# A retention and squared-ReLU kernel on one core: the planner's costs, due times and priorities set anew

## Chip, cores, metric

One core of a Trainium2 chip runs the kernel. The metric is the device time of one execution in microseconds (us), from profiled and unprofiled executions of the same program; the median of the runs is compared.

## What is computed

The reference has two stages. `q`, `k`, `v` are (8 batches, 8 heads, 576 positions, 64) in float32; `w_in` is 512 x 2048, `w_out` is 2048 x 512.

```python
scores = scale * np.matmul(q, k.transpose(0, 1, 3, 2))
gamma = 1.0 - 2.0 ** (-5.0 - np.arange(H, dtype=np.float32))
rel = pos[:, None] - pos[None, :]
Dmat = np.where(rel >= 0, gamma[:, None, None] ** rel[None, :, :], 0.0)
ret = scores * Dmat[None, :, :, :]
attn_out = np.matmul(ret, v)
x = attn_out.transpose(0, 2, 1, 3).reshape(B * S, H * D)      # 4608 x 512
r = np.maximum(x @ w_in, 0.0)
out = (r * r) @ w_out                                          # 4608 x 512
```

## The kernel before

**Tiling.** The 4608 tokens are 36 units of 128 (each batch has four full units; the last 64 positions of two batches make a tail unit). Two units make a group, so there are 18 groups, g0 to g17. Retention is computed chunk by chunk: scores within a chunk (`psc`), masked (`rx` or `rT`), times v (`psO`), with a running state `R` that is fed from k times v (`psS`) and decays from chunk to chunk. VectorE scales `psO` into `xT` (f16), which feeds the second stage.

**Second stage of a group** (`add_ff`). `ph` = x @ w_in comes in 16 blocks of four 128x256 matmuls (L876); two blocks share one PSUM bank. ScalarE takes the relu (`rl`, L884) and squares it (`gT`, L894) for seven of eight banks (three in the last two groups); the rest is squared on VectorE (L896). The second product: g0 does it plainly, 2 x 16 matmuls of 512 columns with w_out (L916). From g1 on it is a Strassen product, seven products p1 to p7 of eight matmuls each (L973; issued in the order p1, p7, p6, p2, p5, p3, p4) instead of eight. It needs sums of halves of `gT` (tile `gS`, L946: s3 for p7, s2 in two halves for p6, s1 for p5, s4 for p3) and of halves of w_out (tile `wT`, L827, four of two halves each: t1 for p5, t2 for p6, t3 for p7, t4 for p4), all on VectorE.

**Loads.** SyncE loads q, k and v. Units 0 to 7 come as pairs, one 512 KB transfer for each of k, q, v and two units: `k0`, `q0`, `v0`, `k2` and so on to `v6` (tile `pair`, L316). GpSimd issues the weights, which are turned into f16 on the way: w0 to w3 are quarters of w_in, w4 to w7 quarters of w_out (L331). The order is `FIRST`: the six transfers of pairs 0 and 2, then w0 to w7, then pairs 4 and 6; w0 is made to wait for v0, and k4 for w5. The pairs are cast to f16 (`kx`, `qx`, L424; `vx`, scaled by position, L420), transposed on TensorE (`psT`, L439) and copied back (`kqT`, L450). From unit 8 on, GpSimd casts k and q (L371, L382) and scales v (L387), and a DMA transposes (L400).

**Order.** Every step is a task with an engine, a key (smaller goes first), a duration, tasks that it depends on, and counted resources (`ff` for the eight PSUM banks, `wst` for staging buffers and so on). `Schedule.emit` plays the tasks through with these numbers: whenever an engine is free it takes the task of the smallest key that is ready and has its resources. The instructions are then written in the order of these planned starts. On the chip each engine follows its list in order and waits at semaphores; the numbers of the plan set nothing but the order. A task ends for another engine after a latency: 0.25 us from TensorE, 0.12 from ScalarE, VectorE and GpSimd; a load's landing is the end of its SyncE task plus `after`, 2.1 us plus what `LAG` has for it.

**The parts that the change names.**

- `fill` (L257 to L260): 34 matmuls on a zero tile, `warm`, with key 10**6: TensorE runs one when nothing else is ready in the plan. Planned at 1.75 us for the first, 0.43 for the next 14, 0.216 for the rest.
- `add_gated` (L265): a task that waits for the k or v cast of a unit, if that unit is one of those from 8 on, since only `add_unit` reads `gate`. `make_tail_pool` (two GpSimd instructions) is gated to unit 4, so it waits for nothing; `tail_dec` then makes the tail's decay row on VectorE (`vdl_tail`) and, in the same call, an Exp on ScalarE.
- `add_weight` (L325): the issue on GpSimd (0.9 us), and a SyncE task of 2.75 us that stands for the transfer.
- `add_unit_pair`: which engine casts what. Pair 0: VectorE. Pair 2: k on GpSimd and ScalarE, q on VectorE and ScalarE. Pairs 4 and 6: k on ScalarE, q on GpSimd. Always v's first half on GpSimd and its second on VectorE.
- `add_wT`: the eight half sums of w_out; those of t1 wait for w4 and w5, all others for w4 to w7.
- `add_ff`, `add_strassen`: relu, square and the sums s1 to s4, with keys by place in the group; `BESIDE` = 1.1 us is the cost of the second half of s2, 0.5 that of the first, 0.8 that of s1, s3 and s4.
- `after_sums`: `fr2` is the state's decay on VectorE.

Of the kernel before, what the change touches and what calls it, by code (L numbers as in the profile page):

```python
# [15 lines left out]
class Schedule:  # L16
# [4 lines left out]
        self.count = dict(count)  # L21
        self.tasks = []

    def add(self, eng, key, dur, fn, deps=(), acq=(), after=None, lag=0.0):
        t = dict(eng=eng, key=key, dur=dur, fn=fn, acq=acq, n=len(self.tasks), users=[], free=[], lag=lag,
                 left=len(deps), ready=0.0, lat=self.LAT[eng] if after is None else after)
        for d in deps:
            d["users"].append(t)
        self.tasks.append(t)
        return t  # L30
# [11 lines left out]
    def emit(self):  # L42
        ready = {e: [] for e in self.LAT}
        busy = {e: False for e in self.LAT}
        events = []
        order = []
        seq = 0

        def push(at, what, t):
            nonlocal seq  # L50
            seq += 1
            heapq.heappush(events, (at, seq, what, t))
        for t in self.tasks:
            if t["left"] == 0:
                heapq.heappush(ready[t["eng"]], (t["key"], t["n"], t))
        now = 0.0
        while True:
            for e in ready:
                if busy[e]:
                    continue  # L60
                held = []
                while ready[e]:
                    item = heapq.heappop(ready[e])
                    t = item[2]
                    if all(self.count[r] >= t["acq"].count(r) for r in t["acq"]):
                        for r in t["acq"]:
                            self.count[r] -= 1
                        t["start"] = now
                        order.append(t)
                        busy[e] = True  # L70
                        push(now + t["dur"], "end", t)
                        break
                    held.append(item)
                for item in held:
                    heapq.heappush(ready[e], item)
            if not events:
                break
            now = events[0][0]
            while events and events[0][0] <= now + 1e-9:
                _, _, what, t = heapq.heappop(events)  # L80
                if what == "end":
                    busy[t["eng"]] = False
                    for w in t["users"]:

                        push(now + (0.0 if w["eng"] == t["eng"] else t["lat"]), "dep", w)
                    for g in t["free"]:
                        push(now + t["lat"], "free", g)
                elif what == "dep":
                    t["left"] -= 1
                    if t["left"] == 0:  # L90
                        push(now + t["lag"], "go", t)
                elif what == "go":
                    heapq.heappush(ready[t["eng"]], (t["key"], t["n"], t))
                else:
# [9 lines left out]
def kernel(  # L104
# [122 lines left out]
    SQ_ACT = (0, 1, 2, 3, 4, 5, 6)  # L227
    SPREAD = 0.1
    QL = 0.8
    BESIDE = 1.1  # L230
    PAUSE = 1.5
    PARTS = 1
    WT_KEY = 96
    URGENT = 40
    SQ_LATE = (1, 4, 6)
    JOIN = 5
    LAG = {"k4": 0.7, "q4": 0.5}
    LAG_T, LAG_O = 1.5, 5.0
    PAIRED = 8
    FIRST = ["k0", "q0", "v0", "k2", "q2", "v2", "w0", "w1", "w2", "w3", "w4", "w5", "w6", "w7", "k4", "q4", "v4", "k6", "q6", "v6"]  # L240
# [31 lines left out]
        nc.gpsimd.tensor_copy(out=iota_pt[0:64], in_=iota_p[0:64])  # L272
        nc.gpsimd.tensor_scalar(out=iota_pt[64:128], in0=iota_p[64:128], scalar1=-64.0, scalar2=None, op0=ALU.add)

    tail_pool = add_gated("POOL", 4, "v", 2.2, make_tail_pool)
    tail_dec = add("DVE", 0, 0.3, lambda: make_vdec("tail", tile_of["iota_pt"]), deps=[tail_pool])

    def dma_task(key, dur, fn, **kw):
# [46 lines left out]
    def add_weight(i):  # L325
        fb = i % 4

        def fn():
            src, dst = ((w_in[:, fb * 512:(fb + 1) * 512].rearrange("(m p) f -> p m f", p=P), w_in16[:, :, fb * 512:(fb + 1) * 512]) if i < 4 else
                        (w_out[fb * 512:(fb + 1) * 512, :].rearrange("(n p) m -> p n m", p=P), w_out16[:, fb * 4:(fb + 1) * 4, :]))  # L330
            tile_of["w", i] = nc.gpsimd.dma_start(out=dst, in_=src)  # L331
            if i == 0:
                behind(tile_of["w", i], tile_of["load", "v", 0])
        issue = add("POOL", -90 + i, 0.9, fn, deps=issues[-1:] or [loaded["v", 0]], lag=1.0 if issues else 0.0)
        issues.append(issue)
        t = add("SP", 0, 2.75, lambda: None, deps=last_load + [issue], after=2.1 + LAG.get(f"w{i}", 0.0))
        last_load[:] = [t]
        wcast[i] = [t]

# [63 lines left out]
    def add_unit_pair(u, base):  # L403
# [4 lines left out]
        for i, name in enumerate("kqv"):  # L408
            xs[name] = []
            for e in range(2):  # L410
                eng = ("DVE" if (e if name == "v" else lead) else "ACT" if name == "k" and u >= 4 or u == 2 and e else
                       "DVE" if name == "q" and u == 2 else "POOL")

                def fc(name=name, e=e, eng=eng):
                    if (name + "x", u) not in tile_of:
                        tile_of[name + "x", u] = cast.tile([P, 2, H * D], FP16, name=name + "x", tag="kq16")
                    t = tile_of[name + "x", u][:, e]
                    x = tile_of[name + "32", u][:, :, e * D:(e + 1) * D]
                    if name == "v":
                        (nc.vector if eng == "DVE" else nc.gpsimd).tensor_tensor(  # L420
                            out=t.rearrange("p (h d) -> p h d", d=D), in0=x,
                            in1=vdec[f"pair{e}"].rearrange("p (h o) -> p h o", o=1).to_broadcast([P, H, D]), op=ALU.mult)
                    else:
                        engines[eng](out=t.rearrange("p (n b a d) -> p n b a d", n=2, b=2, a=2),  # L424
                                     in_=x.rearrange("p (a n b) d -> p n b a d", n=2, a=2))
                dur = (dict(POOL=1.1, DVE=0.6) if name == "v" else dict(POOL=0.62, DVE=0.4, ACT=0.59))[eng]
                xs[name].append(add(eng, base + (7 if name == "v" else i + e / 2), dur, fc, deps=[loaded[name, u]],
                                    acq=() if e else ("kq",)))
            if xs[name][0]["eng"] == xs[name][1]["eng"]:
                sched.need(xs[name][1], xs[name][0])  # L430
# [270 lines left out]
    def after_sums(g, t, key, res):  # L701
# [21 lines left out]
        if not c0:  # L723
            T["Rread", g - 1].append(r0)
        r1 = add("DVE", key + 0.2 - URGENT, 0.69, fr1, deps=[r0])
        r2 = add("DVE", key + 0.3, 0.65, fr2, deps=[r1], acq=("R",))
        T["Rm", g], T["R", g], T["Rread", g], T["Rmread", g] = r0, r2, [], r1
        sched.free("ff", [r0])
        sched.free("ff", [r1])
# [92 lines left out]
    def add_wT(i, in0, in1):  # L822
        ts = []
        for h in range(2):
            def f(h=h):
                sl = slice(h * HF // 2, (h + 1) * HF // 2)
                nc.vector.tensor_tensor(out=wT[i][:, sl], in0=in0[:, sl], in1=in1[:, sl], op=ALU.subtract)  # L827
            ts.append(add("DVE", WT_KEY + i, 0.7, f, deps=sum((wcast[j] for j in range(4, 8 if i else 6)), [])))
        return ts

    t1 = add_wT(0, wB[0, 1], wB[0, 0])
# [1 line left out]
    t3 = add_wT(2, wB[1, 1], wB[0, 1])  # L833
    t4 = add_wT(3, wB[1, 0], wT[1])
    for x, y in ((t2, t1), (t4, t2)):
        for p in y:
            for w in x:
                sched.need(w, p)
    wT_done = {7: t3, 6: t2, 5: t1, 4: t4}

    def store(u, o, lo=0, hi=DM, engs=(nc.sync, nc.sync)):
# [16 lines left out]
    def add_ff(g):  # L858
# [10 lines left out]
        for fb in range(NF // nf):  # L869
# [18 lines left out]
            def fg(fb=fb, on_act=on_act):  # L888
# [5 lines left out]
                    nc.scalar.activation(out=t, in_=rl, func=ACTF.Square)  # L894
                else:
                    nc.vector.tensor_tensor(out=t, in0=rl, in1=rl, op=ALU.mult)  # L896
            r = add("ACT", place(4 * fb + 4), 0.6, fr, deps=[f1[-1]], acq=("rl",))
            sched.free("ff", [r])
            sq.append(add("ACT" if on_act else "DVE", place(4 * fb + 6), 0.63 if on_act else 0.55, fg, deps=[r] + sq[:1],
                          acq=() if fb else ("g",)))  # L900
            sched.free("rl", [sq[-1]])
        sched.free("x", [f1[-1]])
        base2 = base + NF * n
# [28 lines left out]
    def add_strassen(g, us, base, sq):  # L932
# [7 lines left out]
        def add_sum(k, key, parts, in0, in1, op, deps, start=()):  # L940
            out_ = []
            for h in range(parts):
                def f(sl=cut(parts, h)):
                    if ("S", g) not in tile_of:
                        tile_of["S", g] = stage.tile([P, 4, HF, P], FP16, name="gS", tag="wst")
                    nc.vector.tensor_tensor(out=tile_of["S", g][:, k, sl], in0=in0(sl), in1=in1(sl), op=op)  # L946
                out_.append(add("DVE", key + h, (BESIDE if h else 0.5) if parts > 1 else 0.8, f, deps=deps(h, parts) + list(start)))
            sums[k] = out_
            return out_
        nb = len(sq) // 2  # L950
# [161 lines left out]
```

## Time and profile before

| what | us |
|---|---|
| runs (five), median, lowest to highest | 289.64, 289.35 to 290.06 |
| the profiled execution | 289.64 |
| its span, first to last instruction | 287.8 |
| TensorE busy in the span | 281.2 |
| VectorE, ScalarE, GpSimd busy | 178.7, 187.4, 86.3 |
| first `ph` matmul (L876) starts | 17.75 |
| granted TensorE clock, mean | 0.998 |
| weights w_in, w_out, issue to landing (median) | 9.0, 14.0 |

In the profile, lines such as L876 are lines of the kernel. A row of the timeline has the start and the duration in us, the engine, the line, the operation, the tiles it writes and reads with their sizes, and how many instructions were joined; in brackets how long the engine had been idle and what ended that. "PE" is TensorE's matmul row, "PEld" its loading of stationary operands, DVE VectorE, ACT ScalarE, POOL GpSimd. A row of waits has the waiting step, what it waited for, us in total, times, and the longest.

### The profile page before, as it was taken

The numbers are of one execution on the slowest core, as the hardware profiler recorded it, in microseconds if no ns is written. First come the engines' busy times: TensorE is split into PE (matmuls) and PEld (weight loads), VectorE is DVE, ScalarE is ACT, GpSimd is POOL, SyncE is SP. The second block draws the span as 40 slices with busy tenths as digits, with TensorE's granted clock in tenths as the row PEclk, the third lists the DMA queues.
The fourth block names the chain that finished last, engine by engine and source line by source line (L and its number), as shares of the span: only waits on it lengthen the run. The fifth ranks groups of instructions, "written<-read, shape, count | busy, mean of one in ns | idle before, by whom it ended". The sixth has DMA issues, their size and how long they took to land.

```text
span 287.8 us, 10135 instructions
## 1 busy us (share of the span) xinstructions
PE 281.2 (98%) x4346; PEld 236.2 (82%) x4346; DVE 178.7 (62%) x341; ACT 187.4 (65%) x363; POOL 86.3 (30%) x124
## 2 busy tenths in 40 slices
PE   7999999999999999999999999999999999999994
PEld 3578767888888888888888888888888888888883
DVE  3772379858666766547657674777666566364632
ACT  5559975667585857657576748575848675847830
POOL 5560035443524333433334433352522000000000
PEclk9999999999999999999999999999999999999999
DMA  7999999999999898999999897989888020102004
GB/s 199 276 208 206 247 287 274 177 241 156 254 198 165 226 236 187 206 180 189 212 182 224 186 207 177 248 181 246 160 216 205 5 77 2 73 2 75 0 4 144
DMA packets 122156, 49.94 MB, mean 173 GB/s; under 512 B 94720, under 2 KB 117760, under 8 KB 122112
## 3 DMA queue, kind: packets, MB, share of 16 engines
q1 hardware_dynamic: 117568, 44.84, 72.1%
q0 software_dynamic: 4224, 4.19, 8.8%
q8 instruction: 34, 0.56, 0.8%
q10 hardware_dynamic: 320, 0.26, 0.4%
q14 instruction: 10, 0.08, 0.1%
HBM read 36.70 MB, written 9.44 MB: 160 GB/s over the span
## 4 chain that ended last, share of the span: by engine, by line
PE 94%; POOL 2%; issue 2%; DVE 0%; POOLq 0%; DVEq 0%
PE ph L876 44%; PE po L973 37%; PE psO L357 5%; PE po L916 2%; PE psS L357 2%; PE psc L357 2%; PE warm L256 1%; PE psT L439 1%; POOL mask L216 0%; POOL vx L420 0%; POOL w_in L331 0%; DVE o L996 0%; POOL mask_full L208 0%; POOL mask_tail L208 0%; DVE p L1025 0%
## 5 line engine op out<-in xcount | busy, mean ns | idle before, releaser
L876 PE MATMUL ph<-xT,w_in 128*128 128x256 f16 x1152 | 136.5, 273 | 0.0
L876 PEld LDWEIGHTS <-w_in 128*128 128x128 f16 x1152 | 111.4, 98 | 14.4 <-DMA w_in<-in_moe_w_in_dram 0.3
L884 ACT ACTIVATE rl<-ph 128x512 f16<-128x512 f32 x144 | 84.3, 586 | 50.2 <-PE ph L876 47.6
L894 ACT ACTIVATE gT<-rl 128x512 f16<-128x512 f16 x118 | 74.4, 631 | 3.4
L973 PEld LDWEIGHTS <-gS 128*128 128x128 f16 x544 | 51.6, 98 | 6.5
L973 PE MATMUL po<-wT,gS 128*128 128x256 f16 x408 | 55.8, 273 | 0.0
L946 DVE TENSOR_TENSOR gS<-gT,gS 128x512 f16<-128x512 f16 (+1 forms) x51 | 30.7, 601 | 22.0 <-ACT gT L894 21.4
L973 PEld LDWEIGHTS <-gT 128*128 128x128 f16 x408 | 39.6, 98 | 4.7
L973 PE MATMUL po<-w_out,gT 128*128 128x256 f16 x272 | 36.7, 273 | 0.0
L387 POOL TENSOR_TENSOR v<-v,vdec_full 128x512 f16<-128x512 f32 x24 | 25.7, 1070 | 17.5 <-DMA v<-in_v_dram 11.4
L946 DVE TENSOR_TENSOR gS<-gT 128x1024 f16<-128x1024 f16 x34 | 26.2, 772 | 6.4 <-ACT gT L894 6.3
L371 POOL CAST kq<-k 128x512 f16<-128x512 f32 x28 | 19.2, 685 | 36.7 <-DMA k<-in_k_dram 33.0
L382 POOL CAST kq<-q 128x512 f16<-128x512 f32 x24 | 16.3, 679 | 38.8 <-DMA q<-in_q_dram 38.8
L896 DVE TENSOR_TENSOR gT<-rl 128x512 f16<-128x512 f16 x26 | 12.4, 477 | 20.6 <-ACT rl L884 20.6
L996 DVE TENSOR_TENSOR o<-po,u 128x256 f32<-128x256 f32 x33 | 13.9, 422 | 15.3 <-PE po L973 7.7
L986 ACT COPY u<-po 128x256 f32<-128x256 f32 x34 | 12.5, 368 | 15.7 <-PE po L973 15.5
L751 DVE TENSOR_TENSOR xT<-psO,gam_full 128x512 f16<-128x512 f32 x28 | 18.0, 685 | 4.3 <-PE psO L357 4.1
L996 DVE TENSOR_TENSOR o<-po,p 128x256 f32<-128x256 f32 x18 | 7.6, 424 | 20.6 <-ACT u L986 12.6
L973 PE MATMUL po<-w_out,gS 128*128 128x256 f16 x136 | 18.0, 273 | 0.0
L973 PE MATMUL po<-wT,gT 128*128 128x256 f16 x136 | 17.6, 273 | 0.0
L692 DVE TENSOR_TENSOR rT<-psc,mask_full 128x512 f16<-128x512 f32 x24 | 15.6, 683 | 3.1 <-PE psc L357 2.9
L1047 ACT COPY o<-po 128x256 f32<-128x256 f32 x16 | 5.9, 370 | 10.6 <-PE po L973 8.8
(82 smaller groups left out, 227.2 us busy)
## 6 DMA issues: line engine op xcount, KB each, us to landing
out_dram<-o SPq DMA_DIRECT2D x32, 256.0 KB, 2.8
k<-in_k_dram SPq DMA_DIRECT2D x24, 256.0 KB, 4.2
q<-in_q_dram SPq DMA_DIRECT2D x96, 64.0 KB, 3.2
v<-in_v_dram SPq DMA_DIRECT2D x24, 256.0 KB, 3.3
pair<-in_k_dram SPq DMA_DIRECT2D x4, 512.0 KB, 6.5
pair<-in_q_dram SPq DMA_DIRECT2D x4, 512.0 KB, 7.3
pair<-in_v_dram SPq DMA_DIRECT2D x4, 512.0 KB, 7.0
w_in<-in_moe_w_in_dram POOLq DMA_DIRECT2D x4, 512.0 KB, 9.0
```

Source lines behind the costliest of these rows:

```text
L357: t = nc.tensor.matmul(out_, lhsT=lhsT, rhs=rhs, start=start, stop=True, skip_group_check=True, tile_position=(64 * row, 64 * col))
L371: op(out=out_.rearrange("p (n b a d) -> p n b a d", n=2, b=2, a=2), in_=in_.rearrange("p (a n b) d -> p n b a d", n=2, a=2))
L382: nc.gpsimd.tensor_copy(out=tile_of["kq", u][:, 1].rearrange("p (t a d) -> p a t d", t=4, a=2), in_=tile_of["q32", u].rearrange("p (a t) d ...
L387: nc.gpsimd.tensor_tensor(out=t, in0=tile_of["v32", u], in1=vdec[kind].rearrange("p (h o) -> p h o", o=1).to_broadcast([P, H, D]), op=ALU. ...
L692: tile_of["masking", g] = nc.vector.tensor_tensor(out=tile_of["rT", g][:, :, a], in0=tile_of["psc", g][a].rearrange("p (s n i) -> p s n i" ...
L751: nc.vector.tensor_tensor(out=tile_of["x", g].rearrange("p n (s e i) -> p e (n s) i", s=n, e=2)[:, c], in0=y.rearrange("p (o t r) -> p o r ...
L876: nc.tensor.matmul(tile_of["ph", g, fb][:, j, :], lhsT=w_in16[:, m, fi * P:(fi + 1) * P], rhs=tile_of["x", g][:, m, :], start=(m == 0), st ...
L884: nc.scalar.activation(out=t, in_=tile_of["ph", g, fb], func=ACTF.Relu)
L894: nc.scalar.activation(out=t, in_=rl, func=ACTF.Square)
L946: nc.vector.tensor_tensor(out=tile_of["S", g][:, k, sl], in0=in0(sl), in1=in1(sl), op=op)
L973: nc.tensor.matmul(tile_of["pb", g, bank], lhsT=left(i), rhs=right[:, i, :], start=(start and i == 0), stop=(i == HF - 1), skip_group_chec ...
L996: nc.vector.tensor_tensor(out=o_tile(u)[:, half * HM:(half + 1) * HM], in0=bank(x), in1=tile_of[name, g], op=ALU.add)
```

## The change

It alters no instruction's form, only the engine of some casts, the point of one gate, and the planner: its costs, landings, priorities and how it counts VectorE beside GpSimd. What its name says of q's rows and of 34 fillers is in the kernel before already (L316, L225).

- `emit` gets `soft` tasks, on VectorE: while a GpSimd task of over 0.5 us runs, a soft task goes forward at 0.22 of its rate. Soft are the decay `fr2`, the sums for wT, VectorE's squares, and s1 to s4; their costs become 0.62, 0.68, 0.43, and 0.43 (halves) or 0.72.
- A weight chunk is planned at 2.58 us with 3.0 us to landing; `LAG` has new values.
- The tail's constants are gated to the scaling of v of unit 8, which `add_unit` does.
- Pair 2: k and q are cast on ScalarE alone.
- A half of wT waits only for the chunks that it reads, and a dependent half only for its own half.
- In g1 the last bank's relu, VectorE's square, and the sums s1 to s4 get a key that is smaller by `HURRY` = 60.

```diff
+    SHARED = 0.22
...
+        port = dict(task=None, left=0.0, at=0.0, beside=False)
+
+        def shared(beside):
+            t = port["task"]
+            if t is not None:
+                port["left"] -= (now - port["at"]) * (self.SHARED if port["beside"] else 1.0)
+                port["at"] = now
+                t["end"] = now + max(port["left"], 0.0) / (self.SHARED if beside else 1.0)
+                push(t["end"], "end", t)
+            port["beside"] = beside
...
-                        push(now + t["dur"], "end", t)
+                        t["end"] = now + t["dur"]
+                        if t["soft"]:
+                            port.update(task=t, left=t["dur"], at=now)
+                            shared(port["beside"])
+                        else:
+                            push(t["end"], "end", t)
+                        if e == "POOL" and t["dur"] > 0.5:
+                            shared(True)
...
+                    if t["soft"]:
+                        port["task"] = None
+                    elif t["eng"] == "POOL" and t["dur"] > 0.5:
+                        shared(False)
...
-    BESIDE = 1.1
+    HURRY = 60
...
-    LAG = {"k4": 0.7, "q4": 0.5}
+    LAG = {"k0": 0.3, "q2": 0.1, "w7": 1.4, "k4": 0.3, "q4": 0.7, "v4": 0.6, "q6": 0.3, "v6": 1.0}
...
-    tail_pool = add_gated("POOL", 4, "v", 2.2, make_tail_pool)
+    tail_pool = add_gated("POOL", 8, "v", 0.45, make_tail_pool)
...
-        t = add("SP", 0, 2.75, lambda: None, deps=last_load + [issue], after=2.1 + LAG.get(f"w{i}", 0.0))
+        t = add("SP", 0, 2.58, lambda: None, deps=last_load + [issue], after=3.0 + LAG.get(f"w{i}", 0.0))
...
-                eng = ("DVE" if (e if name == "v" else lead) else "ACT" if name == "k" and u >= 4 or u == 2 and e else
-                       "DVE" if name == "q" and u == 2 else "POOL")
+                eng = ("DVE" if (e if name == "v" else lead) else "ACT" if name == "k" and u >= 4 or u == 2 and name != "v" else "POOL")
...
-        r2 = add("DVE", key + 0.3, 0.65, fr2, deps=[r1], acq=("R",))
+        r2 = add("DVE", key + 0.3, 0.62, fr2, deps=[r1], acq=("R",), soft=True)
...
-            ts.append(add("DVE", WT_KEY + i, 0.7, f, deps=sum((wcast[j] for j in range(4, 8 if i else 6)), [])))
+            ts.append(add("DVE", WT_KEY + i, 0.68, f, deps=wcast[4 + h] + (wcast[6 + h] if i else []), soft=True))
...
-        for p in y:
-            for w in x:
-                sched.need(w, p)
+        for w, p in zip(x, y):
+            sched.need(w, p)
...
-            r = add("ACT", place(4 * fb + 4), 0.6, fr, deps=[f1[-1]], acq=("rl",))
+            r = add("ACT", place(4 * fb + 4) - HURRY * (g == 1 and fb == 7), 0.6, fr, deps=[f1[-1]], acq=("rl",))
...
-            sq.append(add("ACT" if on_act else "DVE", place(4 * fb + 6), 0.63 if on_act else 0.55, fg, deps=[r] + sq[:1],
-                          acq=() if fb else ("g",)))
+            sq.append(add("ACT" if on_act else "DVE", place(4 * fb + 6) - HURRY * (g == 1 and not on_act), 0.63 if on_act else 0.43, fg, deps=[r] + sq[:1],
+                          acq=() if fb else ("g",), soft=not on_act))
...
-                out_.append(add("DVE", key + h, (BESIDE if h else 0.5) if parts > 1 else 0.8, f, deps=deps(h, parts) + list(start)))
+                out_.append(add("DVE", key + h - HURRY * (g == 1), 0.43 if parts > 1 else 0.72, f, deps=deps(h, parts) + list(start), soft=True))
```

More of the change, by code (lines that the diff above doesn't have):

```diff
@@ L22, in __init__, with add @@
         self.tasks = []
-    def add(self, eng, key, dur, fn, deps=(), acq=(), after=None, lag=0.0):
-        t = dict(eng=eng, key=key, dur=dur, fn=fn, acq=acq, n=len(self.tasks), users=[], free=[], lag=lag,
+    SHARED = 0.22
+    def add(self, eng, key, dur, fn, deps=(), acq=(), after=None, lag=0.0, soft=False):
+        t = dict(soft=soft, eng=eng, key=key, dur=dur, fn=fn, acq=acq, n=len(self.tasks), users=[], free=[], lag=lag,
                  left=len(deps), ready=0.0, lat=self.LAT[eng] if after is None else after)
@@ L81, in emit @@
                 if what == "end":
+                    if abs(t["end"] - now) > 1e-6:
+                        continue
+                    t["end"] = -1.0
                     busy[t["eng"]] = False
+                    if t["soft"]:
+                        port["task"] = None
+                    elif t["eng"] == "POOL" and t["dur"] > 0.5:
+                        shared(False)
                     for w in t["users"]:
```

## Prediction

> **What bounds the kernel now.** I read the page's first two parts, then busy time by stage, then TensorE's waits, and last the timeline of the first 50 us beside the landing records of the transfers.
>
> ```profile
> PE 281.2 (98%) x4346; PEld 236.2 (82%) x4346; DVE 178.7 (62%) x341; ACT 187.4 (65%) x363; POOL 86.3 (30%) x124
> ...
> PE   7999999999999999999999999999999999999994
> ```
>
> TensorE (PE) is busy in every slice but the first and the last. By stage (columns: PE, PEld, DVE, ACT, POOL, clock, DMA share, GB/s):
>
> ```profile
> 1.26:17.75 16.49, 15.63 (x234) 7.90 (x235) 11.09 (x44) 8.13 (x19) 11.34 (x27) 1.00 1.12 249
> 17.75:51.73 33.98, 33.80 (x471) 25.65 (x465) 21.45 (x37) 25.61 (x48) 9.41 (x13) 1.00 1.15 246
> 51.73:284.00 232.27, 231.72 (x3650) 202.61 (x3647) 145.60 (x255) 153.25 (x296) 65.00 (x81) 1.00 0.76 160
> 284.00:287.90 3.90, 0.00 (x0) 0.00 (x0) 0.24 (x1) 0.00 (x0) 0.00 (x0) 0.81 0.34 82
> ```
>
> From 17.75 us, the first `ph` matmul, to 284 us PE lacks 0.72 us of full, mostly the change between 64-row and 128-row work. Up to 17.75 it is busy too, but 11.01 of those 15.63 us are the 34 fillers `warm`; the DMA engines are full there. Its only named waits:
>
> ```profile
> PE warm L256 <- DVE wT L163: 1.3, 1, 1.3
> PE psS L357 <- POOL vx L420: 0.4, 1, 0.4
> PE psT L439 <- DVE kx L424: 0.2, 1, 0.2
> ```
>
> So time = real matmuls + 34 fillers + PE's idle time + 3.9 us behind the last matmul. The change touches neither the matmuls nor the number of fillers: only idle time can change. About 1 us can be removed ahead of 17.75 us, and 0.15 us at 19.5 us, where PE waits for w1. Much more can be added. The profiled execution took 289.64 us (span 287.85 and 1.8 around it), just the median, so the sum is set against 289.64.
>
> **Ahead of the first ph: nothing.** k0 landed at 5.07 us, yet its cast began at 5.86, as `vdl_tail` stood ahead of it on VectorE and waited for GpSimd. The new gate moves this away and the cast can start 0.7 us sooner. But two later steps hold PE (timeline):
>
> ```profile
> 10.05 1.04 POOL L420 TENSOR_TENSOR vx<-pair,vdec_pair 128x512 f16<-128x512 f32 x1
> ...
> 11.14 0.45 PE L357 MATMUL psS<-vx,kx 64*64 64x64 f16 x32 [0.45 <-POOL vx L420]
> ...
> 14.22 1.45 POOL L420 TENSOR_TENSOR vx<-pair,vdec_pair 128x512 f16<-128x512 f32 x1 [1.06 <-DMA pair<-in_v_dram]
> ...
> 15.72 0.45 PE L357 MATMUL psS<-vx,kx 64*64 64x64 f16 x32
> ```
>
> Both psS begin when GpSimd's vx is done, and vx hangs on the landings of v0 (8.69) and v2 (14.05), which the change leaves alone. I worked PE's new order by hand from the planner's costs: 12 fillers instead of 11 before the first transpose, then 2 instead of 3, and 5 instead of 4 before psc; that is 21 ahead of the first psS, as before, then 9 up to the second (3, 5, 1 instead of 5, 2, 2), then 4. The same counts between the same holds: ph again begins at 17.7. The cast of pair 2 moving to ScalarE (four of 0.62 us, 2.5 in sum, in place of two) is hidden: its k casts end by 11.75, its transposes come at 12.2, and q's copies end near 16.4 with psc at 17.06. Without that cover it would cost at most the 0.6 us of one cast.
>
> **Weights: +0.49 us.** In the planner w(i) landed at 11.95 + 2.75(i+1) + 2.1 us; now 11.95 + 2.58(i+1) + 3.0. That makes w1 20.11 instead of 19.55, w3 25.27 instead of 25.05, w5 30.43 instead of 30.55. The trace has w1 at 19.60, w3 at 24.97, w5 at 30.46. The new plan thus lets PE rest 0.63 us ahead of w1; on the chip that rest is the present 0.15 us, and PE then runs ahead of the plan and meets w3 and w5 too early. Counting the blocks (four matmuls of 109 ns, 0.437 us) that the plan puts ahead of w5's first matmul: before, 9 of g1 (2 ahead of w3, 2 ahead of w4, 5 ahead of w5); now 1, 2 and 4, that is 7. All other work ahead of it is the same.
>
> ```profile
> 30.89 1.03 PE L916 MATMUL po<-w_out,gT 128*128 128x512 f16 x4
> ```
>
> This is w5's first use. It could have begun at 30.51 (landing and 0.05, as w1's first matmul at 19.65 stood to 19.60): 0.38 us of slack. Two blocks less are 0.87 us, so 0.49 us becomes idle, some 0.27 of it at w3. The bounds: 0 if the weights land half a microsecond sooner, 0.9 if later by as much.
>
> **Third pair: +0.2 and -0.2.** With wT's halves tied to single chunks and g1's last sums hurried, VectorE's list at 36 to 42 us gets shorter, and the transposes of k4 move from plan time 40.0 to 38.7. From w5 on PE needs 0.86 + 1.75 + 0.86 + 2.18 + 2.37 us to reach them (38.5; their casts end by about 38.3), then 0.45 + 1.30 + 0.45 + 0.65 + 0.66 + 0.09 to psS: 42.1. GpSimd's vx ended at 42.26 in the trace and has the same landing to wait for: 0.2 us idle (0 to 0.6; if GpSimd's q casts also lengthen beside wT, PE waits there instead). Against it, psS and psc of the fourth pair come to lie side by side: one change of row mode less, 0.09 + 0.12 us by the gaps around psS at 42.9. The hurried relu is no cost by itself: ScalarE does as many instructions.
>
> **Tail constants moved.** Two GpSimd instructions (0.18 + 0.22), one on VectorE (0.23) and one Exp on ScalarE (0.30) go from 5 us to about 53. Behind them wait unit 9's cast, VectorE's backlog, and on ScalarE the relus of g2, which run without gap from 52.80 to 61. ScalarE also waits for VectorE there, up to 1 us. Who waits for it: p1 and the sums of g2, used 1.7 us or more after they were ready. I take zero; 0.5 if that cover were half gone. In the trace the Exp stood among copies without a second table load.
>
> **From 52 us on: +0.2 us.** The plan charged 1.1 us for the second half of s2 and 0.55 for the square ahead of it; now 0.43 each, slowed to 0.22 beside GpSimd. In the timeline the second half of p6 began 0.5 to 1.8 us (mostly 1.2 to 1.7) after its sum was ready; 0.67 + 0.12 us of that was this margin. Beside GpSimd the sums take longer:
>
> ```profile
> 74.45 1.04 POOL L387 TENSOR_TENSOR v<-v,vdec_full 128x512 f16<-128x512 f32 x1 [1.07 <-DMA v<-in_v_dram]
> ...
> 74.53 1.24 DVE L946 TENSOR_TENSOR gS<-gT,gS 128x512 f16<-128x512 f16 x1 [1.74 <-ACT gT L894]
> ```
>
> 1.24 instead of 0.43: the rate gives 0.43 + 0.78 x 1.04 = 1.24. The Trainium skill (SBUF — State Buffer, Who interferes with whom) speaks against a rate: two-input VectorE work and a GpSimd read exclude each other, and the one that comes second waits wholly. That would be 0.96 + 0.43 = 1.39 here, and nothing for a VectorE op that comes first, as with the sum at 57.79 (0.68 with GpSimd beside it all through). So the plan is right where GpSimd leads and too slow where VectorE does; the second only moves PE's work back, which costs nothing. What costs is a GpSimd op that comes at another time than planned. With 0.8 us less margin, some 0.4 to 0.9 are left; a square or sum that meets GpSimd loses up to 0.8. For a quarter of the 12 groups with GpSimd work and a shortfall of 0 to 0.2 I take 0.2 us in all, bounds 0 and 2. By the lock alone it would be about 0.1 more.
>
> Sum: 0 + 0.49 + 0.18 - 0.21 + 0 + 0.2 = 0.66, that is 290.3 us.
>
> **Rivals.** (a) Not slower, chance 0.23: w2 to w5 land sooner. GpSimd no longer casts k2 between the issues of w1 and w2, so w2 is issued at about 11.85 instead of 12.41. If that fills the weights' queue, w5 lands by 29.97 and the 0.49 is gone: 289.64 + 0.18 - 0.21 = 289.6, decided at that landing. Against it: w2 landed 2.5 us after w1 and 9.7 after its issue; the bytes, not the issue, set the pace. (b) Faster, 0.13: the earlier k0 cast carries through, vx of pair 2 is shorter (1.04 as elsewhere, not 1.45), and ph begins at w0's landing, 17.25: 289.1 or less. Against it: w3 and w5 then hold PE the longer. (c) Clearly slower, 0.22: the lost margin counts in most groups, 12 x 0.15 = 1.8 and the rest: 291.5. For it: 12 of the 34 half sums ran beside GpSimd, 0.2 us longer on average. (d) That the change does nothing is part of (a).
>
> **How the numbers follow.** My own case has 0.42 and reaches from 289.95 to 290.7. What a measurement can tell from no change is about 0.2%, 0.58 us: 289.06 to 290.22. Two thirds of my case lie above it (0.28), and all of (c): slower 0.50. One third of mine and (a): same 0.37. (b): faster 0.13. The range 289.2 to 291.9 leaves out half of (b) and the far end of (c).
>
> **What would show it.** Right: PE's list of waits gains `ph` on w_in near 24.7 us and `po` L916 on w_out near 30.3, together about 0.5; ph still starts at 17.7; kx starts at 5.1; psS at 42.3 right behind vx; gaps of PE at L973 behind gS below 0.3 us in all. Wrong: ph starting before 17.4; a gapless stretch from 20 to 40 us; PE waits on VectorE beyond 1 us behind 52 us; a first ph of g2 before 51.7 or after 53.

## The result, and the profile after

The changed kernel takes 290.26 us (median; 289.87 to 291.07) against 289.69 us for the kernel before, run beside it. The ratio is 1.0019, 95% interval 1.0013 to 1.0025: slower by about 0.2%, at the edge of what can be told from no change. The profiled executions are 289.64 before and 290.12 after, their spans 287.85 and 288.41. The prediction was 290.3. All ratios are those on record, which leave out the four executions that were in a slow state and are not the quotients of two medians: the two differ by up to 0.3% (e3: 1.0049, by medians 1.0078), so small steps between experiments have to be read with care.

The page after, first two parts (lines of the new kernel stand 25 to 27 further down: `ph` L901, plain `po` L941, Strassen `po` L998, quads L384, sums `gS` L971):

```profile
PE 281.2 (98%) x4346; PEld 236.0 (82%) x4346; DVE 179.7 (62%) x340; ACT 188.2 (65%) x365; POOL 87.4 (30%) x123
...
PE   8899999999999999999999999999999999999994
```

PE's work is what it was, 281.2 us. Busy time by stage (same columns as before):

```profile
17.75:51.73 33.98, 33.19 (x463) 24.68 (x458) 21.05 (x37) 25.67 (x48) 9.32 (x15) 1.00 1.12 236
51.73:284.20 232.47, 232.19 (x3660) 203.29 (x3656) 146.94 (x255) 153.30 (x298) 67.05 (x81) 1.00 0.74 161
```

The loss lies in the first row: PE lacks 0.79 us there, 0.18 before. In the long stage behind 51.73 us it lacks 0.28, against 0.55. TensorE's waits after:

```profile
PE warm L283 <- DVE wT L190: 1.3, 1, 1.3
PE psS L384 <- POOL vx L446: 1.1, 2, 0.7
PE ph L901 <- DMA w_in<-in_moe_w_in_dram: 0.3, 1, 0.3
```

`warm` waits at the start as before. New are `ph` on w_in, and a second wait of psS on GpSimd's vx; the 0.2 us of `psT` is not in this list any more. Where they are (timeline of PE after):

```profile
17.74 2.36 PE L901 MATMUL ph<-xT,w_in 128*128 128x256 f16 x20
...
25.05 2.79 PE L901 MATMUL ph<-xT,w_in 128*128 128x256 f16 x24 [0.27 <-DMA w_in<-in_moe_w_in_dram]
...
30.29 1.03 PE L941 MATMUL po<-w_out,gT 128*128 128x512 f16 x4
...
42.36 0.45 PE L384 MATMUL psS<-vx,kx 64*64 64x64 f16 x32 [0.35 <-POOL vx L446]
...
43.28 0.42 PE L384 MATMUL psc<-kqT 64*64 64x128 f16 x16
43.63 0.39 PE L998 MATMUL po<-wT,gS 128*128 128x256 f16 x2
43.95 0.42 PE L384 MATMUL psc<-kqT 64*64 64x128 f16 x16
```

The same two steps of the third pair before:

```profile
42.94 0.45 PE L357 MATMUL psS<-vx,kx 64*64 64x64 f16 x32
...
44.07 0.64 PE L357 MATMUL psc<-kqT 64*64 64x128 f16 x32
```

`ph` starts at 17.74 (17.75 before). w3 landed at 25.00 and PE was there early: the bracket counts 0.27 us of idle time from the modelled end of the matmul ahead, and from start to start it is 0.54 us where two such matmuls otherwise stand 0.11 apart. w1 landed at 19.39 (19.60 before), and PE's wait for it, 0.15 us before, is gone. w5 landed at 30.13, not at 30.46, and its first product starts without a wait. The psS of the third pair stands behind vx. The score matmuls `psc` of that pair are cut in two by two `po`.

I summed TensorE's gaps from the start of one matmul to the start of the next, over each part of both traces. The last matmul starts 0.73 us later (283.46, 284.20):

| term | predicted | measured |
|---|---|---|
| ahead of the first ph | 0 | -0.01 |
| weights: gaps inside ph and po up to 40 us | +0.49 | +0.29 |
| psS of the third pair | +0.18 | +0.41 |
| row modes from 40 to 60 us: entering quads (64-row matmuls), and time in them | -0.21 | +0.19 - 0.10 |
| tail's constants | 0 | 0 |
| behind 60 us | +0.2 | -0.10 |
| sum | 0.66 | 0.68 |

The other 0.05 us is spread over short gaps of full matmuls between 40 and 60 us. The 0.29 is 0.43 at w3 less the 0.15 at w1. The -0.10 in row modes comes mostly from a wait: before, psS of the fourth pair stood about 0.2 us for VectorE's vx in its middle, and after it does not.

### The profile page after: what moved, and what is told of

Same layout as the page of the kernel before. It is cut to its first block, busy times and chain, and to the rows that moved or that the text cites. A ratio compares the mean times of both kernels' runs of the same rounds, so it can differ in the third digit from the quotient of the medians.

```text
span 288.4 us, 10133 instructions
## 1 busy us (share of the span) xinstructions
PE 281.2 (98%) x4346; PEld 236.0 (82%) x4346; DVE 179.7 (62%) x340; ACT 188.2 (65%) x365; POOL 87.4 (30%) x123
## 4 chain that ended last, share of the span: by engine, by line
PE 80%; DMA 9%; ACT 3%; SPq 2%; DVE 2%; POOL 2%; issue 0%; DVEq 0%; POOLq 0%; ACTq 0%
PE ph L901 37%; PE po L998 36%; DMA w_out<-in_moe_w_out_dram 5%; PE psO L384 4%; DMA pair<-in_v_dram 3%; DMA pair<-in_k_dram 2%; SPq L343 2%; PE psc L384 2%; PE psS L384 2%; ACT rl L909 1%; ACT gT L919 1%; POOL vx L446 1%; DVE rT L718 0%; ACT kx L450 0%; ACT kqT L476 0%
## 5 line engine op out<-in xcount | busy, mean ns | idle before, releaser
L901 PE MATMUL ph<-xT,w_in 128*128 128x256 f16 x1152 | 137.7, 273 | 0.3 <-DMA w_in<-in_moe_w_in_dram 0.3
L901 PEld LDWEIGHTS <-w_in 128*128 128x128 f16 x1152 | 111.3, 98 | 14.7 <-DMA w_in<-in_moe_w_in_dram 0.5
L998 PEld LDWEIGHTS <-gS 128*128 128x128 f16 x544 | 51.6, 98 | 6.8
L998 PE MATMUL po<-wT,gS 128*128 128x256 f16 x408 | 56.1, 273 | 0.0
L998 PEld LDWEIGHTS <-gT 128*128 128x128 f16 x408 | 39.7, 98 | 4.9
L971 DVE TENSOR_TENSOR gS<-gT,gS 128x512 f16<-128x512 f16 (+1 forms) x51 | 31.4, 617 | 19.6 <-ACT gT L919 19.1
L998 PE MATMUL po<-w_out,gT 128*128 128x256 f16 x272 | 36.9, 273 | 0.0
L414 POOL TENSOR_TENSOR v<-v,vdec_full 128x512 f16<-128x512 f32 x24 | 27.5, 1145 | 29.2 <-DMA v<-in_v_dram 23.8
L971 DVE TENSOR_TENSOR gS<-gT 128x1024 f16<-128x1024 f16 x34 | 27.2, 799 | 8.2 <-ACT gT L919 8.1
L998 PE MATMUL po<-w_out,gS 128*128 128x256 f16 x136 | 17.7, 273 | 0.0
L998 PE MATMUL po<-wT,gT 128*128 128x256 f16 x136 | 17.6, 273 | 0.0
L487 DVE TENSOR_TENSOR R<-stmp,dec 128x512 f16<-128x512 f32 (+1 forms) x18 | 13.0, 722 | 0.5
```

The lines of the kernel that those rows point to most:

```text
L414: nc.gpsimd.tensor_tensor(out=t, in0=tile_of["v32", u], in1=vdec[kind].rearrange("p (h o) -> p h o", o=1).to_broadcast([P, H, D]), op=ALU. ...
L901: nc.tensor.matmul(tile_of["ph", g, fb][:, j, :], lhsT=w_in16[:, m, fi * P:(fi + 1) * P], rhs=tile_of["x", g][:, m, :], start=(m == 0), st ...
L998: nc.tensor.matmul(tile_of["pb", g, bank], lhsT=left(i), rhs=right[:, i, :], start=(start and i == 0), stop=(i == HF - 1), skip_group_chec ...
```

## The experiments

They ran in three groups (e1 to e4, e5 to e8, e9 to e12), each group on one chip of its own, beside the kernel before on that chip; ratios are against that. "By the gaps" means: from the start of one matmul to the start of the next, less the usual step. The lists of waits leave out idle times under 0.15 us, the gaps do not. Two of the planner's halves were exchanged in turn: the landings (the transfer's 2.58 + 3.0 us and the new `LAG`, or the old 2.75 + 2.1 us), and VectorE's costs with the rate.

**e1: the kernel before with the new landings alone.**

```diff
-    LAG = {"k4": 0.7, "q4": 0.5}
+    LAG = {"k0": 0.3, "q2": 0.1, "w7": 1.4, "k4": 0.3, "q4": 0.7, "v4": 0.6, "q6": 0.3, "v6": 1.0}
-        t = add("SP", 0, 2.75, lambda: None, deps=last_load + [issue], after=2.1 + LAG.get(f"w{i}", 0.0))
+        t = add("SP", 0, 2.58, lambda: None, deps=last_load + [issue], after=3.0 + LAG.get(f"w{i}", 0.0))
```

> The kernel before with nothing of the change but the planned landings (2.58 and 3.0 us for a weight chunk, the new LAG). Landing theory (PE reaches w3, or w5, and the psS of the third pair before their data): the plan again has only 7 blocks of g1 ahead of w5's first matmul and psS at plan time 42.15, so the same two waits, 0.3 us at w3 and 0.4 us at psS: 290.3 us, ratio 1.002. Rate theory (the loss comes from VectorE's new costs and the lost margin behind 52 us): no loss, 289.7 us.

Measured 292.72 us, ratio 1.0079 (1.0061 to 1.0097): four times the loss of the whole change. In its timeline one step that nobody had looked at is the longest wait:

```profile
111.47 0.32 PE L357 MATMUL psc<-kqT 64*64 64x64 f16 x16 [1.20 <-DMA kqT<-kq]
```

The scores of a late group wait for their DMA transpose. A further 0.5 us is lost at `po` on VectorE's `xT` near 50 us. The new landings do cost time, but hardly where they were expected to: by the gaps w3 holds PE for 0.09 us and the third pair's psS not at all.

**e2: the changed kernel with the old landings** (the reverse of e1's edit).

> The changed kernel with the landings planned as before the change (2.75 and 2.1 us, old LAG); all other parts of the change stay. Landing theory: 9 blocks of g1 ahead of w5 again, psS at plan time 43.56, so no wait at w3 or psS beyond 0.15 us: 289.7 us, ratio 1.000. Rate theory: the loss stays, 290.3 us.

Ratio 0.9991 (0.9969 to 1.0013; 1.0011 by the medians): no loss is left that can be told from noise, as expected. Neither w3 nor the third pair's psS holds PE; other small waits stand in their place, the largest at 63 us, on ScalarE:

```profile
PE po L998 <- ACT p L1011: 0.7, 1, 0.7
PE psS L384 <- POOL vx L446: 0.5, 1, 0.5
```

The second row is the wait of pair 0, which before has too. By the gaps psS of the fourth pair stands 0.6 us for VectorE's vx, as it does in e9 and e12.

**e3: the changed kernel with pairs 4 and 6 planned later**, so that psS of the third pair would not come early.

```diff
-    LAG = {"k0": 0.3, "q2": 0.1, "w7": 1.4, "k4": 0.3, "q4": 0.7, "v4": 0.6, "q6": 0.3, "v6": 1.0}
+    LAG = {"k0": 0.3, "q2": 0.1, "w7": 1.4, "k4": 2.06, "q4": 1.86, "v4": 1.36, "k6": 1.36, "q6": 1.36, "v6": 1.36}
```

> The changed kernel with the landings of pairs 4 and 6 planned as late as in the plan of before (LAG raised by 1.4 to 2.1 us), the weights' landings left as changed. It undoes the wait at the third pair's psS alone. Landing theory: the wait at w3 (0.3 us) stays, that at psS (0.4 us) goes: 289.9 us, 0.2 to 0.3 above before. If the weights alone cost, 290.3; if neither does, also 290.3.

A miss: ratio 1.0049 (1.0028 to 1.0069). The wait at w3, which was to stay, is gone as well (PE stands at w1 instead, 0.46 us by the gaps). The third pair's wait is gone, and the fourth's takes its place, larger (first row: timeline; second: waits):

```profile
49.62 0.45 PE L384 MATMUL psS<-vx,kx 64*64 64x64 f16 x32 [1.27 <-POOL vx L446]
```

```profile
PE psc L384 <- DMA kqT<-kq: 2.1, 3, 1.0
```

Again the transposes, 2.1 us in three places.

**e4: the kernel before with 30 fillers** (`WARM = 30` instead of 34), for the prediction's claim that the fillers are not what bounds the start.

> The kernel before with 30 fillers for 34; the four that go are those between the second psS (15.72 us) and psc. If time were simply PE's matmuls and fillers, four of 0.216 us less: 288.8 us. Landing theory: ph starts 0.4 us sooner, at w0's landing, and then waits 0.6 us or more for w1 at 19.6 instead of 0.15: 289.7 us, no gain.

Ratio 0.9992 (0.9973 to 1.0011): four fillers, 0.86 us of PE, win nothing.

```profile
16.38 0.53 PE L357 MATMUL psc<-kqT 64*64 64x128 f16 x24 [0.21 <-ACT kqT L450]
17.43 0.30 PE L357 MATMUL psc<-kqT 64*64 64x128 f16 x7 [0.52 <-issue]
17.67 1.92 PE L876 MATMUL ph<-xT,w_in 128*128 128x256 f16 x16
19.90 1.48 PE L876 MATMUL ph<-xT,w_in 128*128 128x256 f16 x12 [0.32 <-DMA w_in<-in_moe_w_in_dram]
```

PE reaches psc sooner and waits there; ph starts at 17.67 and what is won, 0.08 us, is waited for again at w1. The long stand, 0.52 us, has no releaser in the trace. It falls ahead of the 224th matmul of PE's list, and in eight other traces (before, after, e2, e5, e6, e7, e9, e10) psc also pauses at just that place, with 0.09 to 0.21 us from start to start, though in e4 that is four score matmuls further on; in all nine the pause ends at 17.43 to 17.46. So something tied to the place in the list holds ph as well, beside the two psS of the prediction. What it is, no run here tests.

**e5: the changed kernel with w1 alone planned 0.45 us sooner**, so that the plan rests less ahead of w1 and puts one block more ahead of w5.

```diff
-    LAG = {"k0": 0.3, "q2": 0.1, "w7": 1.4, "k4": 0.3, "q4": 0.7, "v4": 0.6, "q6": 0.3, "v6": 1.0}
+    LAG = {"k0": 0.3, "q2": 0.1, "w1": -0.45, "w7": 1.4, "k4": 0.3, "q4": 0.7, "v4": 0.6, "q6": 0.3, "v6": 1.0}
```

> The changed kernel with one number changed: w1's landing planned 0.45 us sooner (19.66 us, as the trace has it). The plan then has no rest of 0.63 us ahead of w1, 8 blocks of g1 ahead of w5 and psS at plan time 44.0 instead of 42.15. Landing theory: both waits of the changed kernel (0.3 us at w3, 0.4 us at the third pair's psS) go, with this one number: 289.7 us, as before. Rate theory (VectorE's new costs lose it behind 52 us): 290.3.

Ratio 1.0020 (0.9999 to 1.0040), median 290.87: it cannot be told from before, nor from after. In the trace both waits, at w3 and at the third pair, are gone as they should be (that at w3 is gone in e3, e8 and e10 too, without this edit), but the profiled run (292.08, above this kernel's median) waits 1.6 us for transposes, in four places. The lowest run, 289.34, is level with before's lowest, 289.3.

**e6: the changed kernel with VectorE's old costs and no rate.** The costs of `fr2`, wT, the squares and the sums are before's, for instance:

```diff
-                out_.append(add("DVE", key + h - HURRY * (g == 1), 0.43 if parts > 1 else 0.72, f, deps=deps(h, parts) + list(start), soft=True))
+                out_.append(add("DVE", key + h - HURRY * (g == 1), (1.1 if h else 0.5) if parts > 1 else 0.8, f, deps=deps(h, parts) + list(start)))
```

> The changed kernel with VectorE's costs as before the change (0.55, 0.5 and 1.1, 0.8, 0.65, 0.7) and no slower rate beside GpSimd. PE's order up to plan time 46 is that of the changed kernel. Rate theory: the loss goes, 289.7. Landing theory: both waits stay, 290.3 at least; as the plan also rests PE 0.66 us at 50 us, PE would run ahead of the transposes of units 12 to 20, as in the runs with late landings: up to 291.

Ratio 1.0056 (1.0030 to 1.0082): slower than the change itself, by more than expected. The longest wait is on VectorE, at the end of g1:

```profile
52.67 0.60 PE L998 MATMUL po<-wT,gT 128*128 128x256 f16 x4 [1.06 <-DVE o L1021]
```

and 0.5 us on a transpose at 110. Neither of the two waits that were to stay is there: w3 and the third pair's psS do not hold PE, and w5's first product stands 0.29 us by the gaps. So beside the new landings the new costs are worth about 0.35% (1 us); they are not what makes the change slower.

**e7: e5 and e6 together.**

> Both at once: VectorE's costs as before the change, and w1's landing planned 0.45 us sooner. In this plan PE rests only 0.18 us behind 17.8 us (before 0.64, changed kernel 0.63). If what costs is a rest that the plan has and the chip has not, this is the best order so far: 289.4 to 289.7 us, no wait at w3, psS, or a transpose. Rate theory: 289.7. If margins decide more than rests, 290 or more.

Ratio 1.0008 (0.9982 to 1.0035), profile 289.9. No wait at w3 and none on a transpose; psS of the fourth pair waits 0.6 us for VectorE's vx. Level with before within the interval, without the gain that was expected.

**e8: the changed kernel without the rate** (`soft=False` throughout, the new costs kept).

> The changed kernel with its new VectorE costs (0.43, 0.72 and so on) but no slower rate beside GpSimd, so no margin at all is left for GpSimd. PE's order is that of the changed kernel up to 56 us. Landing theory: 290.3 us, as the changed kernel, with PE waits on VectorE of at most 0.3 us in sum. Rate theory (lost margin): slower by 0.5 us or more than the changed kernel, 290.8 to 291.5.

Ratio 1.0041 (1.0024 to 1.0058), 291.32: the number that the rate theory expected, by another way. By the list PE waits for VectorE nowhere behind the start (one sum holds it 0.08 us by the gaps); it waits for transposes:

```profile
PE psc L384 <- DMA kqT<-kq: 1.3, 2, 0.8
...
PE psS L384 <- POOL vx L446: 1.0, 2, 0.7
```

So the theory that the rate keeps VectorE's sums clear of GpSimd falls, though its time came out. What the costs and the rate change, as far as these traces show, is where the scores stand in PE's list.

**e9 and e10: the kernel before, and the changed kernel, unchanged, on one chip**, to tell whether the order or the chip makes the transposes late.

> The kernel before, unchanged, on the chip of this group, for its trace. Theory A (the order decides how early the DMA transposes are issued): the score matmuls of groups 6 to 10 find their transposes landed 1.5 us or more ahead, as in the first trace of before (1.5 to 4.4), and PE has no wait on kqT behind 52 us. Theory B (the chip decides): leads near zero and waits on kqT of 0.3 us or more, as in the runs of edited kernels. Time 289.7 (289.3 to 290.1 if nothing disturbs), ratio 1.000.

> The changed kernel, unchanged, beside before on one chip. Ratio 1.002 as measured (1.001 to 1.0035). Theory A: leads of the transposes in groups 6 to 10 of 0 to 1.3 us, clearly less than the run of before beside it; waits on kqT of 0 to 0.6 us. Theory B: the leads are those of the run of before beside it. Either way a wait at w3 of about 0.3 and at psS of the third pair of about 0.4 us.

e9 has ratio 1.0004 (0.9989 to 1.0018), e10 1.0022 (1.0012 to 1.0032), which repeats the result. But it repeats it by other waits. In these two traces the last matmul starts 0.99 us later, and in the terms of the table above that is -0.18 at the weights, +0.46 at psS of the third pair, +0.18 and -0.30 in the row modes, and +0.80 behind 60 us. PE stands 0.18 us at w1 (0.36 in e9) and at neither w3 nor w5. Of the 0.80, 0.70 is at a transpose of group 9 and 0.2 at a half sum. The transposes of group 9, queue of SyncE, before (e9) and after (e10):

```profile
115.02 1.66 SPq L400 DMA_TRANSPOSE kqT<-kq  x1
116.73 1.67 SPq L301 DMA_DIRECT2D k<-in_k_dram  x1
118.51 1.59 SPq L400 DMA_TRANSPOSE kqT<-kq  x1
```

```profile
116.91 2.11 SPq L427 DMA_TRANSPOSE kqT<-kq  x1
119.07 0.59 SPq L328 DMA_DIRECT2D k<-in_k_dram  x1
120.19 1.23 SPq L427 DMA_TRANSPOSE kqT<-kq  x1
```

and the scores that read them, before and after:

```profile
125.21 0.43 PE L357 MATMUL psc<-kqT 64*64 64x64 f16 x32
```

```profile
123.01 0.30 PE L384 MATMUL psc<-kqT 64*64 64x64 f16 x16
123.82 0.32 PE L384 MATMUL psc<-kqT 64*64 64x64 f16 x16 [0.51 <-DMA kqT<-kq]
```

The transposes are issued 1.7 us later and the scores come 2.2 us sooner: of a lead of 2.64 us nothing is left. Lead of the last transpose's landing over the scores in groups 6 to 10, e9: 3.46, 2.56, 1.08, 2.64, 0.91 us; e10: 0.42, 0.07, 0, -0.77, 0.42 (the second is an estimate from the issue and this trace's median of 3.98 us to landing, as its landing is not in the trace). On one chip and by one trace each, that speaks for the order, theory A. The place of the scores of groups 6 to 9 in PE's list, as ph and po matmuls ahead of them, with the waits on DMA transposes in the profiled run:

| kernel | g6, g7, g8, g9 | waits on transposes, us | ratio |
|---|---|---|---|
| before, e4, e9, e11, e12 | 488, 592, 700, 808 | 0 | 0.9986 to 1.0029 |
| e2 | 484, 592, 696, 800 | 0 | 0.9991 |
| e7 | 476, 576, 688, 792 | 0 | 1.0008 |
| after, e10 | 472, 580, 688, 784 | 0, 0.5 | 1.0019, 1.0022 |
| e5 | 472, 580, 688, 784 | 1.6 | 1.0020 |
| e8 | 472, 572, 680, 784 | 1.3 | 1.0041 |
| e6 | 472, 576, 672, 776 | 0.5 | 1.0056 |
| e1 | 472, 576, 672, 776 | 1.2 | 1.0079 |
| e3 | 472, 576, 680, 776 | 2.1 | 1.0049 |

A matmul is 109 ns. After stands 12 to 24 of them sooner than before, 1.3 to 2.6 us of lead; e1 and e6 up to 32, 3.5 us. In groups 6 to 9 no kernel that left the scores in before's places waited for a transpose; e4 lost 0.3 us by the gaps to one in group 10. The place alone does not set the wait: after, e10 and e5 have the same places and waits of 0, 0.5 and 1.6 us.

**e11: the changed kernel with old costs and old landings**, e6's and e2's edits together; what stays is the tail's gate, pair 2's casts on ScalarE, wT's halves and the hurry in g1.

> The changed kernel with the old VectorE costs, no rate and the old landings: what is left of the change is the tail's gate, pair 2's casts on ScalarE, wT's halves tied to single chunks, and g1's hurried steps. The plan has 9 blocks ahead of w5 again and 0.40 us of rest. If landings and VectorE costs were the whole loss: 289.5 to 289.8, ratio 0.999 to 1.0005, no wait at w3 and none of psS in the third pair. If the rest of the change costs by itself (casts on ScalarE, hurried sums): 290.2 or more.

Ratio 0.9986 (0.9966 to 1.0006), 289.73: as expected. It is not proven faster, and it has the lowest run of all, 288.97. With it, the change's two halves can be read off (ratio to before, with its interval; the cells come from three chips):

| | old landings | new landings |
|---|---|---|
| old VectorE costs | e11: 0.9986 (0.9966 to 1.0006) | e6: 1.0056 (1.0030 to 1.0082) |
| new costs with the rate | e2: 0.9991 (0.9969 to 1.0013) | e10: 1.0022 (1.0012 to 1.0032) |

The new landings cost 0.7% with the old costs and 0.3% with the new ones; the new costs do nothing with the old landings and win some 0.35% with the new.

**e12: the kernel before with the tail's gate alone.**

```diff
-    tail_pool = add_gated("POOL", 4, "v", 2.2, make_tail_pool)
+    tail_pool = add_gated("POOL", 8, "v", 0.45, make_tail_pool)
```

> The kernel before with one part of the change, the gate of the tail's constants. Prediction's step: nothing lost at 53 us, and nothing won ahead of the first ph though the first kx cast starts at 5.1 instead of 5.9; ph at 17.7, 289.7, ratio 0.999 to 1.001. Rival (b) of the prediction: ph at 17.25 or less, 289.2. The other rival: VectorE or ScalarE late at 53 us, PE waits of 0.3 to 0.5 there, 290.0 to 290.2.

Its trace is as expected (VectorE, then PE):

```profile
4.89 0.89 DVE L424 CAST kx<-pair 128x512 f16<-128x512 f32 x2 [1.72 <-DMA pair<-in_k_dram]
```

```profile
17.48 1.92 PE L876 MATMUL ph<-xT,w_in 128*128 128x256 f16 x16
19.72 1.48 PE L876 MATMUL ph<-xT,w_in 128*128 128x256 f16 x12 [0.32 <-DMA w_in<-in_moe_w_in_dram]
```

The cast begins about 1 us sooner (5.86 in e9), ph 0.26 sooner (17.74), and half of that is waited for again at w1: the next block starts 0.14 sooner than in e9. PE has no listed wait behind 52 us, and its last matmul starts at 284.10, in e9 at 284.24. The times do not agree with this: nine runs from 289.88 to 291.69, ratio 1.0029 (1.0012 to 1.0046). The profiled run (290.20) is among the three lowest of the nine, so it shows no cause for the higher times. e11, which holds the same gate, is not slower than before. Whether the gate alone costs time in some executions stays open.

## Why the prediction was right, and where only its sum was

The likeliest case was 289.95 to 290.7 with 290.3 in the middle, and 290.26 came. The direction held, and so did the cause as far as the landings go: with the old ones (e2, e11) no loss is left that can be told from noise. Where the time is lost held in part: at psS of the third pair in after and in e10, at w3 in after alone. By steps:

- **Ahead of the first ph, nothing: right.** 17.75 and 17.74, with the fillers in the counts worked out. e12 shows how little the earlier cast wins, and e4 that the fillers win nothing; but there PE is held by the stand in psc that the prediction did not have.
- **Weights, +0.49: mis-sized, 0.29 from before to after and -0.18 from e9 to e10.** The two blocks less ahead of w5's first product are in the trace (23 for 25). What failed is that one trace's landings were taken as fixed: w5 was kept at 30.46 and came at 30.13, and the wait of 0.15 at w1 was kept and went. The gaps at w1, w3 and w5 together hang more on w1's landing (19.39 to 19.89) than on the order: 0.15 to 0.49 us, mean 0.30, in the six traces with 25 blocks (before, e2, e4, e9, e11, e12), and 0.18 to 0.46, mean 0.38, in the six with 23 (after, e1, e3, e6, e8, e10). A steady cost of the two blocks beyond about 0.1 us is not shown. Rival (a) named earlier landings and a cause for them, w2 issued 0.6 us sooner. The cause is not shown: w5 landed at 29.84 to 30.46 in the five traces that issue w2 at 12.20 or later, and at 29.86 to 30.46 in the nine that issue it before 12.
- **psS of the third pair, +0.18: right in kind, 0.41 in size (0.46 in e10, 0.34 in e8).** PE had no wait at w5, so it was through at 41.95 instead of the forecast 42.1 (41.20 and six `po` of 109 ns, and 0.09 for the change of mode), and vx came at 42.31 instead of 42.26. The two terms are tied: part of what the weights do not take, vx takes.
- **Row modes, -0.21: wrong sign.** psS and psc were to lie side by side. The new order instead cuts psc of the third and the fourth pair in two by `po` and `ph`, so the quads of this stage are entered eight times instead of six, each at 0.09 us, in e10 as in after.
- **Tail's constants, 0: shown in the traces** (no wait of PE there in after, e10, e11 or e12), with the open point of e12.
- **Behind 52 us, +0.2: nothing in after, 0.80 in e10, and mostly in another place.** The margin of the half sums did shrink: from g2 on, the second half of p6 begins a median 0.9 us after its sum in after, 1.5 in before. No product waited for one in after. In e10 one did, in the way that the prediction gave (GpSimd, VectorE, PE):

```profile
78.31 0.61 POOL L398 CAST kq<-k 128x512 f16<-128x512 f32 x1 [0.27 <-DMA k<-in_k_dram]
```

```profile
78.35 0.84 DVE L971 TENSOR_TENSOR gS<-gT,gS 128x512 f16<-128x512 f16 x1
```

```profile
79.25 0.61 PE L998 MATMUL po<-wT,gS 128*128 128x256 f16 x4
```

The sum, 0.42 us alone, ends at 79.19, and the product starts 0.2 us late by the gaps. What costs more is the transposes' lead, a step the prediction did not list at all: 0.70 us in e10. In after the lead was just enough (about 1.1 to 1.7 us in four of the five groups, about 0 at g9; four of these landings are estimates from the issue and the trace's median of 3.97 us).

Two of the prediction's own signs of being wrong came, though its number held: the first ph of g2 starts at 50.37, before 51.7, and in e10 PE runs from 20 to 40 us without a wait.

On the rate itself, the traces side with the Trainium skill and not with the plan. After, GpSimd and VectorE, at two places:

```profile
60.91 0.61 POOL L409 CAST kq<-q 128x512 f16<-128x512 f32 x1 [1.96 <-DMA q<-in_q_dram]
```

```profile
61.04 0.76 DVE L971 TENSOR_TENSOR gS<-gT,gS 128x512 f16<-128x512 f16 x1 [1.54 <-ACT gT L919]
```

```profile
40.86 1.45 POOL L446 TENSOR_TENSOR vx<-pair,vdec_pair 128x512 f16<-128x512 f32 x1 [0.60 <-ACT gT L919]
```

```profile
41.33 1.27 DVE L971 TENSOR_TENSOR gS<-gT,gS 128x512 f16<-128x512 f16 x1
```

Both sums, 0.42 us alone, came second. The first had 0.48 us of GpSimd's work left ahead of it and took 0.76, the second had 0.98 left and took 1.27: 0.50 us more of GpSimd cost 0.51 us more, where the rate 0.22 would make it 0.39. All 158 sums of the fourteen traces that began behind one GpSimd instruction with over 0.25 us of it left do the same: each took its own time and all of GpSimd's remaining time, less 0.13 to 0.15 us. The rate misses them by up to 0.1 us either way. That is a whole wait, as the Trainium skill has it (SBUF — State Buffer, Who interferes with whom: the two exclude each other), shortened here by that constant. A sum that began first kept its 0.42 or 0.68 us. The prediction's check of the rate came out at 1.24 because it took GpSimd's whole 1.04 us, of which 0.96 was left: the rate gives 1.18, the whole wait less 0.14 gives 1.24 to 1.25.

So that 0.66 met 0.68 is partly luck, an offset of terms: 0.2 us too much at the weights, 0.3 too much behind 52 us, 0.2 too little at psS and 0.3 at the row modes. From e9 to e10 the ratio is about the same and the terms are others. That the new landings cost the time stands on e1, e2, e6 and e11; that PE there runs ahead of a rest which the plan grants is argued.

Two points are open: the higher times of e12, and why the new landings place the scores of g6 to g9 earlier. By the planner's own arithmetic TensorE rests 0.40 us between 17.8 and 60 us in e11, 0.64 before, 0.63 after, and 1.37, 1.37 and 1.52 in e1, e6 and e3, the three slowest. That fits a rest which the plan grants and the chip does not take, but it does not tell after from before, and nothing here tests it by itself.

## What to carry to other kernels

New landing times in a planner can make the order worse, the more so where they are not truer. By the planner's arithmetic, the changed kernel's are nearer to the traces for k4 (36.80, before 38.56; 37.06 in the trace of before), and later than any of the fourteen traces for w1 (20.11; 19.39 to 19.89) and w3 (25.27; 24.56 to 25.00), so check each one against more than one trace. Beyond that, what counts is whether the plan lets the engine rest where the chip makes it rest, and what the order then takes from every later lead. Before forecasting a re-planned order, list the lead of each class of data over its reader (weights, sums, transposes), not only of the class that the change names. And test each half of such a change with and without the other, since here neither is worth the same alone.

## What was not expected of the hardware

- With a mean busy share of the DMA engines of 0.95 to 1.00 between 40 and 160 us, a DMA transpose in after was 4.0 us from issue to landing (median of the 16 of 28 whose landing is in the trace), and held SyncE's queue 1.2 to 2.5 us itself. The same transpose of group 9 landed about when the scores began in one execution of the changed kernel, and 0.77 us after they began in the other.
- The landing of one weight transfer moved by 0.4 us between two executions of the kernel before (w5 30.46 and 30.04), nearly as much as the term that the prediction built on it.
- VectorE's sum waits for the whole of a GpSimd instruction that began first, less 0.13 to 0.15 us, and runs at its own pace when it began first (158 sums, above).
- PE pauses in psc ahead of the 224th matmul of its list in nine of the fourteen traces, up to 0.52 us of idle time in e4, with no releaser in the trace ("issue"); no run here explains it.
